# Two products change places in the order of a three-part matmul kernel, and three transposes move forward

## The chip, the cores and the metric

One core of one Trainium2 chip runs the whole program. The metric is the device time of one execution in microseconds (us); it is the median of several runs. Profiled executions are separate runs with the hardware profiler on, and every time inside the kernel is counted from the first instruction of such an execution.

## The reference

Three layers follow one another on 1536 tokens (2 batches of 768) with 512 features: a decayed linear attention, a mixture of 8 experts whose gate is normalised 8 times, and a dense layer with a leaky activation.

```python
state = gamma * state + einsum('bhd,bhe->bhde', k[:, :, t], v[:, :, t])   # attention, per token t
y[:, :, t] = scale * einsum('bhd,bhde->bhe', q[:, :, t], state)
...
for e in range(E):                                   # 8 experts, D 512, F 1024
    h = np.maximum(x @ w1[e], 0.0)
    out += P[:, e:e + 1] * (h @ w2[e])
...
h = x @ w_in                                         # dense layer, d_ff 2048
g = np.maximum(h, 0.0) + alpha * np.minimum(h, 0.0)
return g @ w_out
```

## The kernel before

After the attention the program is a list of 20 phases (`PHASES`). Phases 0 to 7 are the experts on the first batch. Phases 8 to 15 are the experts on the second batch, and 16 to 19 are the two halves of the dense layer on the first and on the second batch. Phases 8 to 19 are called fast in the code (`FAST`); below they are F1 to F12, so F1 to F8 are experts and F9 to F12 dense halves. The change touches fast phases alone. Each of them computes 1024 hidden units for 768 tokens and multiplies them with a second weight matrix.

The matrix products use a seven-product scheme (Strassen's, in Winograd's form): a 2x2 block product takes 7 products of half size. Each value is split in a high and a low part, so that every block multiplication is three matmuls, `L288`, `L289` and `L290` (`mm3`). A product of the first layer is `product(ph, j, p)`: block column `j` (0 to 3, 256 hidden units each) and product number `p` (1 to 7). It has two such triples, six matmuls of 128x384. The second layer is 28 units `u` (`fast2`), each also six matmuls.

The products of one column share four PSUM banks, A, B, D and E:

- 1 opens A. ScalarE (ACT) then copies A into B (`L934`), and product 6 adds onto that B.
- After 6, ACT copies B into a new bank E (`L934`), and then B into the SBUF block `b21` (`L934` too). Products 5 and, later, 3 add onto E.
- 7 opens D. ACT copies D into the SBUF block `b22` (`L934`), and product 4 later adds onto D.
- 2 adds onto A, and ACT turns A into `b11` (`L954`); 3 ends E, and ACT turns it into `b12` (`L954`). VectorE (DVE) adds E to `b22` after 5 and D to `b21` after 4 (`L949`). In the dense phases ACT writes `n` (`L905`) and DVE joins it (`L906`) in place of a ReLU.

DVE and ACT then make the operands of the second layer: `t1` to `t4` (`L1016`, `L1020`, `L1022`) combine blocks, `hhigh` (`L1042`, ACT) writes the high part of a tile `hs`, and `hlow` (`L1050` or `L1020`/`L1022`, DVE) its low part. There are 14 such `hs` tiles in a phase, and unit `u` reads number `u // 2`.

No scheduler reorders anything. A phase is a list of places (`sequence`): 26 from `fast_order`, then product 4 of column 3, unit 0, product 3 of column 3, and units 1 to 27. All other work is hung on places by number with `step(ph, place, ...)`, or on a product with `at(...)`, and follows that product's own work. So every engine has a fixed order, and each waits for the others by semaphores. All loads and stores are issued from one queue, SP's. The second layer's weights (`ws_load`, tile `ws`, 6 buffers) are loaded when the pair of units six tiles earlier has been issued.

In F1 alone, `turn` transposes the first batch's result (`total`) in eight pieces on TensorE (PE, 3 matmuls each, `L1161`), ACT copies each piece (`L1166`, tile `tt`) and SP stores it. `decode_at` turns weights that arrive as raw 64-bit words (`rd`, a load that SP issues) into floats on DVE (`L832` to `L837`, `L850`, `L853`).

Of the kernel before, what the change touches and what calls it, by code (L numbers as in the profile page):

```python
# [46 lines left out]
def tile_kernel(ctx, tc, lead, qkT, kv, ctab, w_gate, w1, w2, w_in, w_out, alpha, out):  # L47
# [69 lines left out]
    def w1_sum(n, q, eng):  # L117
        if n // NJ in AGAIN:
            return
        r = raw[0, n]  # L120
        s = r[:, 1024:1792].rearrange("p (a b) -> p a b", a=3)
        a11, a12, a22, a21 = (r[:, 256 * i:256 * i + 256] for i in range(4))
        out, in0, in1, op = (
            (s[:, 0], a21, a22, ALU.add),
            (s[:, 1], s[:, 0], a11, ALU.subtract),
            (s[:, 2], a21, a11, ALU.subtract),
            (a21, a12, s[:, 1], ALU.subtract),
        )[q]
        eng.tensor_tensor(out=out, in0=in0, in1=in1, op=op)  # L129

    def w1_adds(n, eng):
        if n < NJ * len(PHASES):
            for q in range(4):
                w1_sum(n, q, eng)

    def w1_high(n, part):
        kept = n // NJ in AGAIN
        if n >= NJ * len(PHASES) or kept and part == "c":
            return
        if part == "a":  # L140
            src, width, pieces = raw[0, n][:, 0:512], 512, (A11, A12)
        elif part == "b":
            width, pieces = (256, (A22,)) if kept else (512, (A22, W4))
            src = raw[0, n][:, 512:512 + width]
        else:
            src, width, pieces = raw[0, n][:, 1024:1792], 768, (W1, W2, W3)
        both = spot(n, part, 2 * width)
        hi, lo = both[:, 0:width], both[:, width:2 * width]
        nc.scalar.activation(out=hi, in_=src, func=AF.Copy)  # L149
        known = ws1.setdefault(n, {})  # L150
        known[part] = (lo, src, hi)
        for q, piece in enumerate(pieces):
            known[piece] = (hi[:, 256 * q:256 * q + 256], lo[:, 256 * q:256 * q + 256])

    def w1_low(n, part, eng):
        if n >= NJ * len(PHASES) or n // NJ in AGAIN and part == "c":
            return
        lo, src, hi = ws1[n].pop(part)
        eng.tensor_tensor(out=lo, in0=src, in1=hi.bitcast(F32), op=ALU.subtract)  # L159
        if part == "b" and n != 2 * NJ * E - 2:  # L160
            w_load(0, n + 2)
        if n < NJ * E and part != "a":
            unkept.append([2, n, part, hi, lo])
# [25 lines left out]
    def w2_high(n):  # L189
        hi, lo = (pools["wq"].tile([128, 1024], F32R, tag=f"v{n % NJ}{w}", name=f"v{n}{w}") for w in "hl")  # L190
        nc.scalar.activation(out=hi, in_=raw[1, n], func=AF.Copy)
        ws2[n] = (hi.rearrange("p (a b) -> p a b", a=2), lo.rearrange("p (a b) -> p a b", a=2))

    def w2_low(n, q, eng):
        hi, lo = (t[:, q, :] for t in ws2[n])
        eng.tensor_tensor(out=lo, in0=raw[1, n][:, 512 * q:512 * q + 512], in1=hi.bitcast(F32), op=ALU.subtract)
        if q == 1:
            w_load(1, n + 2)

    def w2_keep(n):  # L200
        e, j = divmod(n, NJ)
        for q in range(2):
            v = ws2[n][q].bitcast(F32).rearrange("p i (r c) -> p i r c", r=2)
            nc.sync.dma_start(out=c2[e][:, j, 0:2, q, :], in_=v[:, :, 0, :])
            nc.sync.dma_start(out=c2[e][:, j, 2, q, :], in_=v[:, 1, 1, :])
# [191 lines left out]
    with tc.manual_schedule():  # L397

        with ExitStack() as actx:
# [53 lines left out]
            pool, dve = nc.gpsimd, nc.vector  # L453
# [245 lines left out]
            for g in range(1, NST // 2):  # L699
                i = 2 * g  # L700
# [351 lines left out]
        def ws_load(ph, w):  # L1052
            if w >= 14:
                ph, w = ph + 1, w - 14
                if ph in XGROUP:
                    return
            if ph not in FAST:
                return
            x, jp = divmod(w, 2)
            t = wr[ph, w] = pools["fast"].tile([128, 2, 2, 256], F32R, tag="ws", bufs=6, name=f"ws{ph}_{w}")  # L1060
            nc.sync.dma_start(out=t.bitcast(F32), in_=c2[PHASES[ph][1]][:, 2 * jp:2 * jp + 2, PIECE2[ORDER2[x]]])
# [110 lines left out]
        def at(ph, key, *fns):  # L1172
            hooks.setdefault((ph, key), []).extend(fns)

        pool, dve = nc.gpsimd, nc.vector
# [3 lines left out]
        order += [(NJ - 1, 3), (NJ - 1, 4)]  # L1179
        slots = [f"t{t}{w}" for t in range(TT) for w in ("a", "")]  # L1180

        fast_order = [(0, 1), (0, 7), (0, 2), (0, 6), (0, 5)]
        for j in range(1, NJ):
            fast_order += [(j, 1), (j - 1, 4), (j, 2), (j, 6), (j - 1, 3), (j, 7), (j, 5)]

        def sequence(ph):
            if ph in FAST:
# [6 lines left out]
        def step(ph, pos, *fns):  # L1194
            if pos >= 60:
                ph, pos = ph + 1, pos - 60
            for fn in fns:
                at(ph, seq[ph][pos], fn)
# [20 lines left out]
        def w1_at(ph, m, add_eng, eng, adds, ah, al, ch, cl, bh, bl):  # L1219
            step(ph, adds, lambda: w1_adds(m, add_eng))  # L1220
            for part, hi, lo in (("a", ah, al), ("c", ch, cl), ("b", bh, bl)):
                step(ph, hi, lambda part=part: w1_high(m, part))
                step(ph, lo, lambda part=part: w1_low(m, part, eng))

        xk, x3 = [], []
        for ph in range(len(PHASES)):
            n = NJ * ph
# [25 lines left out]
                step(ph, 20, lambda m=n + 4: w1_kept(m))  # L1253
                step(ph, 26, lambda m=n + 5: w1_kept(m))
            if fast:
                w1_at(ph, n + 2, pool, dve, 0, 3, 4, 5, 7, 10, 11)
                w1_at(ph, n + 3, pool, dve, 5, 10, 12, 12, 14, 17, 18)
                w1_at(ph, n + 4, pool, dve, 28 if ph == 2 * E - 1 else 18, 36, 38, 39, 40, 42, 43)
                w1_at(ph, n + 5, pool, dve, 28, 44, 45, 48, 49, 50, 52)
            else:  # L1260
                if ph:
                    w1_at(ph, n + 2, pool, pool, 0, 3, 3, 6, 6, 9, 9)
                    w1_at(ph, n + 3, pool, pool, 5, 10, 10, 12, 12, 16, 16)
                else:
                    step(ph, 0, lambda: w1_adds(2, pool))
                    step(ph, 10, lambda: w1_adds(3, pool))
                    for m, part, hi, lo, eng in (
                        (2, "a", 5, 5, pool), (2, "c", 9, 9, pool), (2, "b", 11, 15, pool),
                        (3, "a", 13, 16, dve), (3, "c", 14, 14, pool), (3, "b", 17, 17, pool),
                        (4, "a", 25, 26, dve), (4, "c", 30, 31, dve), (4, "b", 37, 37, dve),  # L1270
                        (5, "a", 34, 34, dve), (5, "c", 34, 34, dve), (5, "b", 37, 37, dve),
                    ):
                        step(ph, hi, lambda m=m, part=part: w1_high(m, part))
                        step(ph, lo, lambda m=m, part=part, eng=eng: w1_low(m, part, eng))
                    for m, q, pos in ((4, 0, 22), (4, 1, 22), (4, 2, 24), (4, 3, 24), *((5, q, 31) for q in range(4))):
                        step(ph, pos, lambda m=m, q=q: w1_sum(m, q, dve))
                if ph > 0:
                    w1_at(ph, n + 4, dve, dve, 29, 29, 30, 31, 32, 31, 32)
                    w1_at(ph, n + 5, dve, dve, 33, 33, 34, 35, 36, 35, 36)
                early = ((4, 6, 7, dve), (9, 12, 13, dve), (15, 16, 20, dve), (22, 25, 26, dve))  # L1280
                first = ((6, 6, 7, dve), (12, 13, 14, dve), (20, 20, 20, pool), (24, 24, 24, pool))
                for j, (hi, l0, l1, eng) in enumerate(early if ph else first):
                    step(ph, hi, lambda m=n + j: w2_high(m))
                    step(ph, l0, lambda m=n + j, eng=eng: w2_low(m, 0, eng))
                    step(ph, l1, lambda m=n + j, eng=eng: w2_low(m, 1, eng))
                for j, pos in enumerate((19, 22, 29, 31)):
                    step(ph, pos, lambda m=n + j: w2_keep(m))
            if fast:
# [35 lines left out]
                if E < ph < 2 * E - 1:  # L1324
                    for keys in ((12, 17, 18, 27), (37, 39, 41, 45), (46, 48, 50, 55)):
                        i = unit[0] - NJ * E
# [21 lines left out]
        for w in range(6):  # L1348
            for ph in (E, 2 * E, 2 * E + 2):
                at(ph, ((0, 7), (1, 5), (1, 6), (1, 2), (2, 1), (2, 6))[w], lambda ph=ph, w=w: ws_load(ph, w))  # L1350
        for i, pos in enumerate((2, 4, 8, 11, 15, 18, 22, 25)):
            step(E, pos, lambda a=i % 4, h=i // 4: turn(2, a, h))
        def signs():
            dve.tensor_scalar(out=sg, in0=al, scalar1=1.0, scalar2=-2.0, op0=ALU.is_gt, op1=ALU.mult)
# [124 lines left out]
```

## Time and profile before

| | |
|---|---|
| median of 3 runs | 1285.64 us (1284.69 to 1285.79) |
| the profiled execution | 1288.47 us, of which the span from first to last instruction is 1286.7 us |
| PE busy in the span | 1261.4 us (98%) |
| DVE, ACT, POOL busy | 1011.5 us (79%), 659.6 us (51%), 459.5 us (36%) |
| fast phases | from 549.8 us to the end, about 60 to 65 us each |
| granted clock of PE | 0.998 of 2.4 GHz in the mean |

A row of the timeline gives the start of an instruction, its duration, engine, line, operation, output and inputs, and in square brackets the idle time of that engine before it and what ended it. Matmuls are pipelined: one is listed with some 0.33 us, but the next starts about 0.17 us after it. So idle time in brackets counts from the modelled end of the matmul before, and the pitch between starts says more.

### The profile page before, as it was taken

To read this page: it belongs to the slowest core of one execution; us is meant where nothing else is said; L and a number is where in the kernel's file an instruction comes from. 1 tells how busy PE (TensorE), PEld (TensorE's weight loads), DVE (VectorE), ACT (ScalarE), POOL (GpSimd) and SP (SyncE) were. 2 spreads that over 40 slices of the span, in tenths; PEclk is the share of its full clock that TensorE was granted. 3 is DMA by queue.
4 is the path that set the end of the run, shared out by engine and by line. 5 is a ranking of instruction groups with operands and counts; after the bars stand their busy time and mean duration, and the time that the engine had idled before them with its cause. 6 is when DMAs were issued, how large, how long until landed. Compare 5 with 4: busy or idle time off the path is not lost.

```text
span 1286.7 us, 20628 instructions
## 1 busy us (share of the span) xinstructions
PE 1261.4 (98%) x7358; PEld 1190.8 (93%) x7358; DVE 1011.5 (79%) x1546; ACT 659.6 (51%) x1217; POOL 459.5 (36%) x414
## 2 busy tenths in 40 slices
PE   9999999999999999999999999999999999999998
PEld 7889998989898989899999999999999989989998
DVE  6676888888898889758696777768685989797866
ACT  5634544444353535355545454646464556655573
POOL 5743252616170706001143413242322655543200
PEclk9999999999999999999999999999999999999999
DMA  9784999999999999899898989898988976596615
GB/s 359 242 287 134 330 333 343 337 339 337 332 341 343 337 346 334 289 334 350 299 357 277 346 280 342 291 351 280 348 280 293 352 237 207 188 350 221 218 46 180
DMA packets 231158, 379.21 MB, mean 295 GB/s; under 512 B 16992, under 2 KB 135824, under 8 KB 231056
## 3 DMA queue, kind: packets, MB, share of 16 engines
q1 hardware_dynamic: 231056, 377.90, 86.1%
q8 instruction: 58, 0.95, 0.3%
q14 instruction: 44, 0.36, 0.1%
HBM read 243.59 MB, written 132.67 MB: 292 GB/s over the span
## 4 chain that ended last, share of the span: by engine, by line
PE 84%; DVE 7%; DMA 3%; ACT 3%; issue 2%; SPq 0%; POOL 0%; DVEq 0%; ACTq 0%; POOLq 0%
PE B L289 7%; PE B L288 7%; PE o L288 7%; PE o L290 7%; PE B L290 7%; PE o L289 7%; PE A L288 6%; PE A L290 6%; PE A L289 6%; PE D L288 4%; PE D L290 4%; PE D L289 4%; PE E L288 4%; PE E L289 4%; PE E L290 4%
## 5 line engine op out<-in xcount | busy, mean ns | idle before, releaser
L129 POOL TENSOR_TENSOR raw<-raw 128x256 f32<-128x256 f32 x136 | 134.5, 1000 | 99.3 <-DMA raw<-in_w_dram 34.8
L1042 ACT ACTIVATE hs<-b 128x768 fp32r<-128x768 f32 x168 | 140.1, 842 | 58.0 <-DVE b L1020 14.9
L1050 DVE TENSOR_TENSOR hs<-b,hs 128x768 fp32r<-128x768 f32 x120 | 122.2, 1018 | 9.8 <-ACT hs L1042 9.5
L224 POOL TENSOR_TENSOR pr<-pr 128x256 f32<-128x256 f32 x52 | 51.2, 985 | 189.2 <-DMA pr<-in_w_dram 124.9
L149 ACT ACTIVATE W<-raw 128x512 fp32r<-128x512 f32 (+1 forms) x144 | 98.1, 695 | 19.8 <-DVE raw L129 19.3
L288 PE MATMUL A<-xh,W 128*128 128x384 f32 x320 | 108.0, 337 | 0.0
L290 PE MATMUL A<-xh,W 128*128 128x384 f32 x320 | 107.3, 335 | 0.0
L289 PE MATMUL A<-xl,W 128*128 128x384 f32 x320 | 107.1, 335 | 0.0
L357 POOL TENSOR_TENSOR xs<-b,xs 128x384 fp32r<-128x384 f32 x21 | 26.6, 1267 | 208.2 <-ACT xs L353 208.2
L289 PE MATMUL B<-hs,ws 128*128 128x384 f32 x288 | 97.0, 337 | 3.4 <-DVE hs L1050 3.3
L288 PE MATMUL B<-hs,ws 128*128 128x384 f32 x288 | 96.4, 335 | 0.2 <-ACT hs L1042 0.2
L290 PE MATMUL B<-hs,ws 128*128 128x384 f32 x288 | 96.3, 334 | 0.0
L1100 POOL TENSOR_TENSOR total<-total,t 128x384 f32<-128x384 f32 x54 | 69.6, 1318 | 64.6 <-DVE t L1080 61.5
L159 POOL TENSOR_TENSOR W<-raw,W 128x512 fp32r<-128x512 f32 (+1 forms) x49 | 76.3, 1572 | 41.7 <-PE B L290 20.7
L288 PE MATMUL B<-xh,W 128*128 128x384 f32 x268 | 90.8, 339 | 0.2 <-DVE D L972 0.2
L290 PE MATMUL B<-xh,W 128*128 128x384 f32 x268 | 89.7, 335 | 0.0
L289 PE MATMUL B<-xl,W 128*128 128x384 f32 x268 | 89.6, 334 | 0.0
L934 ACT ACTIVATE B<-A 128x384 f32<-128x384 f32 x48 | 22.8, 475 | 129.4 <-PE A L290 129.1
L267 POOL TENSOR_TENSOR dr<-dr 128x256 f32<-128x256 f32 x32 | 41.6, 1301 | 132.7 <-DMA xd<-tt 68.8
L288 PE MATMUL D<-xh,W 128*128 128x384 f32 x236 | 80.9, 343 | 7.7 <-ACT b L934 7.6
L159 DVE TENSOR_TENSOR W<-raw,W 128x512 fp32r<-128x512 f32 (+1 forms) x95 | 85.9, 920 | 2.3 <-ACT W L149 2.3
L949 DVE TENSOR_TENSOR b<-E,b 128x384 f32<-128x384 f32 x48 | 26.7, 556 | 72.4 <-PE E L290 67.5
(495 smaller groups left out, 3998.1 us busy)
## 6 DMA issues: line engine op xcount, KB each, us to landing
ws<-c SPq DMA_DIRECT2D x168, 512.0 KB, 5.9
raw<-in_w_dram SPq DMA_DIRECT2D x64, 512.0 KB, 5.6
c<-W SPq DMA_DIRECT2D x64, 384.0 KB, 6.6
W<-c SPq DMA_DIRECT2D x88, 256.0 KB, 6.0
pr<-in_w_dram SPq DMA_DIRECT2D x32, 512.0 KB, 5.7
c<-pw SPq DMA_DIRECT2D x32, 512.0 KB, 7.1
c<-pr SPq DMA_DIRECT2D x32, 512.0 KB, 7.7
raws<-in_w_dram SPq DMA_DIRECT2D x32, 384.0 KB, 4.8
```

The lines of the kernel that those rows point to most:

```text
L129: eng.tensor_tensor(out=out, in0=in0, in1=in1, op=op)
L149: nc.scalar.activation(out=hi, in_=src, func=AF.Copy)
L159: eng.tensor_tensor(out=lo, in0=src, in1=hi.bitcast(F32), op=ALU.subtract)
L224: eng.tensor_tensor(out=out, in0=in0, in1=in1, op=op)
L267: nc.gpsimd.tensor_tensor(out=out, in0=in0, in1=in1, op=op)
L288: nc.tensor.matmul(ps, ah, bh, start=first, stop=False, skip_group_check=True)
L289: nc.tensor.matmul(ps, ah, bl, start=False, stop=False, skip_group_check=True)
L290: nc.tensor.matmul(ps, alo, bh, start=False, stop=last, skip_group_check=True)
L949: nc.vector.tensor_tensor(out=dst, in0=src, in1=dst, op=ALU.add)
L1042: nc.scalar.activation(out=t[:, 0, :], in_=hsource(ph, k), func=func)
L1050: nc.vector.tensor_tensor(out=lo, in0=src, in1=hi.bitcast(F32), op=ALU.subtract)
L1100: eng.tensor_tensor(out=dst, in0=dst, in1=tt[m, h], op=ALU.add)
```

## The change

In column 0 the products come as 1 7 6 2 5 in place of 1 7 2 6 5. In column 3, product 7 comes ahead of product 3 of column 2, which now stands directly ahead of product 5. (The general line is changed and columns 1 and 2 are put back as they were by the two swaps.) The split of column 2's first weight pieces (those of products 1 and 2) into high and low part moves one place later, from places 3 and 4 to 4 and 5; the place that it writes to is read by column 0's product 2, which now stands at place 3. Places count from 0. In F1, the last three of the eight transposes move from places 18, 22 and 25 to 17, 20 and 22.

```diff
-        fast_order = [(0, 1), (0, 7), (0, 2), (0, 6), (0, 5)]
+        fast_order = [(0, 1), (0, 7), (0, 6), (0, 2), (0, 5)]
         for j in range(1, NJ):
-            fast_order += [(j, 1), (j - 1, 4), (j, 2), (j, 6), (j - 1, 3), (j, 7), (j, 5)]
+            fast_order += [(j, 1), (j - 1, 4), (j, 2), (j, 6), (j, 7), (j - 1, 3), (j, 5)]
+        fast_order[9], fast_order[10] = fast_order[10], fast_order[9]
+        fast_order[16], fast_order[17] = fast_order[17], fast_order[16]
...
-                w1_at(ph, n + 2, pool, dve, 0, 3, 4, 5, 7, 10, 11)
+                w1_at(ph, n + 2, pool, dve, 0, 4, 5, 5, 7, 10, 11)
...
-        for i, pos in enumerate((2, 4, 8, 11, 15, 18, 22, 25)):
+        for i, pos in enumerate((2, 4, 8, 11, 15, 17, 20, 22)):
```

On ACT, at the start of F2 (phase 9 in the names; A, B, D, E are banks, `b_9` the SBUF blocks), the order changes like this:

```order
 L934 ACTIVATE B_6655<-A_6648 128x384
 L934 ACTIVATE b_9_6674<-D_6667 128x384
-L954 ACTIVATE b_9_6682<-A_6648 128x384
-L934 ACTIVATE E_6691<-B_6655 128x384
-L934 ACTIVATE b_9_6693<-B_6655 128x384
-L149 ACTIVATE W<-raws 128x512
...
+L934 ACTIVATE E_6682<-B_6655 128x384
+L934 ACTIVATE b_9_6684<-B_6655 128x384
+L954 ACTIVATE b_9_6693<-A_6648 128x384
+L149 ACTIVATE W<-raws 128x512
```

The two copies out of B after product 6, into E and into `b21`, now come ahead of the ReLU of product 2.

On ACT, at the end of F2's first layer (`hs_1` and `hs_4` are high parts for the second layer, the row with D is the copy into `b22` after product 7, the rows with E are ReLUs after product 3):

```order
 L934 ACTIVATE E_6900<-B_6864 128x384
 L934 ACTIVATE b_9_6819<-B_6864 128x384
-L1042 ACTIVATE hs_4_6903<-b_9_6682 128x768
-L954 ACTIVATE b_9_6911<-E_6817 128x384
+L1042 ACTIVATE hs_4_6903<-b_9_6693 128x768
+L934 ACTIVATE b_9_6835<-D_6905 128x384
 L1042 ACTIVATE hs_1_6913<-b_9_6809 128x768
-L934 ACTIVATE b_9_6835<-D_6915 128x384
-L954 ACTIVATE b_9_6911<-E_6900 128x384
+L954 ACTIVATE b_9_6921<-E_6817 128x384
+L954 ACTIVATE b_9_6921<-E_6900 128x384
```

The copy of D moves ahead of one high part, and the ReLU of column 2's product 3 goes behind it.

On DVE, at the end of F9's first layer (phase 16, a dense one; `n_01` is what ACT writes for product 3, `b_16_11101` is `b22`):

```order
 L906 SCALAR_TENSOR_TENSOR b_16_11079<-b_16_11079,sg,n_10_11141 128x384
-L906 SCALAR_TENSOR_TENSOR b_16_11175<-E_11077,sg,n_01_11176 128x384
-L1050 TENSOR_TENSOR hs_4_11165<-b_16_10914,hs_4_11165 128x768
+L1050 TENSOR_TENSOR hs_4_11165<-b_16_10924,hs_4_11165 128x768
 L949 TENSOR_TENSOR b_16_11101<-E_11160,b_16_11101 128x384
+L906 SCALAR_TENSOR_TENSOR b_16_11186<-E_11077,sg,n_01_11187 128x384
 L1022 TENSOR_TENSOR b_16_11001<-b_16_10904,b_16_11001 128x768
```

The join for column 2's product 3 moves from ahead of the low part of `hs_4` to behind the sum of `b22`.

## Rows read from the trace of the kernel before

**Rows 1.** Windows of F1, F2, F8, F10: length, busy of PE, PEld, DVE, ACT, POOL, clock, DMA share.
```profile
549.80:613.40 63.60, 61.55 (x362) 60.64 (x361) 45.36 (x69) 33.91 (x63) 4.71 (x4) 1.00 1.00 353
613.40:673.30 59.90, 58.95 (x338) 58.30 (x337) 47.64 (x67) 31.80 (x58) 14.96 (x12) 1.00 0.93 327
...
973.00:1036.00 63.00, 59.90 (x339) 58.30 (x338) 49.21 (x64) 31.88 (x56) 28.57 (x23) 1.00 0.84 294
...
1098.00:1163.00 65.00, 61.35 (x337) 59.40 (x336) 55.29 (x69) 38.26 (x69) 29.95 (x28) 0.97 0.76 274
```

**Rows 2.** Waits of PE: who waited for whom, us in total, times, longest.
```profile
PE D L288 <- ACT b L934: 7.6, 11, 1.8
PE E L288 <- ACT E L934: 6.9, 12, 0.6
PE B L289 <- DVE hs L1050: 3.3, 3, 1.7
```

**Rows 3.** Timeline of F2's first products on PE and ACT.
```profile
617.40 0.34 PE L290 MATMUL B<-xh,W 128*128 128x384 f32 x1
...
617.77 0.47 ACT L934 ACTIVATE E<-B 128x384 f32<-128x384 f32 x1 [0.55 <-PE B L290]
...
618.30 0.44 PE L288 MATMUL E<-xh,W 128*128 128x384 f32 x1 [0.56 <-ACT E L934]
...
619.46 0.34 PE L288 MATMUL A<-xh,W 128*128 128x384 f32 x1
...
620.51 0.33 PE L288 MATMUL D<-xh,W 128*128 128x384 f32 x1
```

**Rows 4.** Timeline of F2's last column: ACT, then the matmul that waits.
```profile
639.51 0.85 ACT L1042 ACTIVATE hs<-b 128x768 fp32r<-128x768 f32 x1 [0.21 <-DVE b L1020]
640.27 0.47 ACT L954 ACTIVATE b<-E 128x384 f32<-128x384 f32 x1
640.64 0.84 ACT L1042 ACTIVATE hs<-b 128x768 fp32r<-128x768 f32 x1
641.38 0.48 ACT L934 ACTIVATE b<-D 128x384 f32<-128x384 f32 x1
...
641.91 0.44 PE L288 MATMUL D<-xh,W 128*128 128x384 f32 x1 [0.39 <-ACT b L934]
```

**Rows 5.** Timeline of F1: DVE behind a load, ACT behind DVE, PE.
```profile
572.35 0.43 DVE L832 TENSOR_SCALAR ex<-rd 128x512 uint32<-128x512 uint32 x1 [4.30 <-DMA rd<-in_w_out_dram]
...
579.26 0.85 ACT L1042 ACTIVATE hs<-b 128x768 fp32r<-128x768 f32 x1 [1.56 <-DVE b L1020]
...
582.03 0.44 PE L288 MATMUL D<-xh,W 128*128 128x384 f32 x1 [1.48 <-ACT b L934]
```

**Rows 6.** Timeline of F8 on PE: column 3's product 4, a later unit.
```profile
1000.84 0.34 PE L290 MATMUL E<-xh,W 128*128 128x384 f32 x1
1001.25 0.45 PE L288 MATMUL D<-xh,W 128*128 128x384 f32 x1
...
1030.89 0.45 PE L289 MATMUL B<-hs,ws 128*128 128x384 f32 x1 [1.68 <-DVE hs L1050]
```

**Rows 7.** Timeline of F9: DVE joins product 3, PE starts product 4.
```profile
1064.34 0.62 DVE L906 SCALAR_TENSOR_TENSOR b<-E,sg,n 128x384 f32<-128x384 f32 x1 [0.74 <-ACT n L905]
...
1065.47 0.45 PE L288 MATMUL D<-xh,W 128*128 128x384 f32 x1 [1.12 <-ACT b L934]
```

**Rows 8.** Timeline of F10: PE, DVE, and PE at a late unit.
```profile
1128.19 0.45 PE L288 MATMUL D<-xh,W 128*128 128x384 f32 x1 [1.81 <-ACT b L934]
...
1136.55 0.96 DVE L1050 TENSOR_TENSOR hs<-b,hs 128x768 fp32r<-128x768 f32 x1 [1.08 <-ACT hs L1042]
...
1159.08 0.45 PE L289 MATMUL B<-hs,ws 128*128 128x384 f32 x1 [0.95 <-DVE hs L1050]
```

**Rows 9.** Window of F10, columns as in Rows 1.
```profile
1129.00:1132.00 3.00, 3.00 (x11) 3.00 (x11) 3.00 (x5) 1.23 (x2) 2.92 (x3) 0.50 1.03 410
```

**Rows 10.** Loads of the second layer's weights, all phases: issue to landing.
```profile
DMA to landing us min/median/max: 3.3/5.9/8.8
```

## Prediction

> **What bounds the kernel now.** I read the page first, then a table of windows, one for each fast phase, then the waits of PE, and last the timeline around each wait. In F2's 59.9 us PE is busy 58.95 and DVE 47.64, and the page has PE at 98% with no other engine above 79%; so time can be won only where PE stands still, or runs slowly as in F10, with a mean clock of 0.97 [rows 1]. The waits of PE say where it stands: in two places of nearly every fast phase [rows 2]. The one is a first matmul onto E that waits for ACT's copy into E, 12 times, 6.9 us in all. The other is a matmul onto D that waits for ACT's copy out of D, 11 times, 7.6 us. A third kind, units of the second layer behind DVE, comes 3 times.
>
> The timeline gives the true price of such a wait. In F2 the last matmul of product 6 starts at 617.40 and product 5 starts at 618.30 [rows 3]. Six matmuls take 1.05 (619.46 to 620.51), so the pitch is 0.175, and 0.90 minus 0.175 is 0.73 lost. Product 5 itself then takes 1.16 (618.30 to 619.46) where a product takes 1.05, which is 0.11 more. One wait costs 0.84: the 0.56 of idle in brackets and 0.28 that the bracket does not count. I add 0.27 to every bracket; the 0.39 ahead of F2's product 4 [rows 4] is 0.66.
>
> **The change part by part.**
>
> *Column 0: product 6 ahead of product 2.* Product 5 needs the copy into E. ACT starts it 0.2 after PE is done with product 6, and PE goes on 0.73 after that point [rows 3]. Now product 2 stands between and covers 1.05, so the wait goes and 0.3 is left over. The ReLU of product 2 goes behind the copy on ACT, so nothing new lies ahead of it. The price is on product 6: it adds onto B, ACT's copy of A after product 1. That copy had two products as cover (7 and 2) and now has one, 7. By the timing of the copy into E, 0.73 against 1.05, one is enough. I cost it at nothing; if that cover fell short by the whole, it would be 0.84 again. Gain: 6.9 + 12 x 0.27 = 10.1 us.
>
> *Column 3: product 7 ahead of product 3.* Product 4 waits for the copy of D into `b22`. In F2 that copy is the last of four on ACT: a high part at 639.51 that waited for DVE, the ReLU at 640.27, a second high part at 640.64, the copy at 641.38 [rows 4]. In the new order the copy stands behind the first high part, at about 640.3, and frees D at about 640.8. Without its wait PE would be there at 641.91 - 0.55, about 641.35. So the wait goes, with 0.5 to spare. The second high part stays within 0.1 of its time, and the ReLU that goes behind it is not needed before the next product 3. F2 to F7, F11 and F12 have the same order and no other wait. Their brackets are the 7.6 less the three long ones, 1.48, 1.12 and 1.81 [rows 5, 7, 8], which leaves 3.2 for eight; with 8 x 0.27 that is a gain of 5.35 us.
>
> The other four phases are bound differently at this place.
>
> - F1: DVE stood 4.30 behind a load that landed at 572.35, and ACT's first high part waited for DVE until 579.26 [rows 5]. The window's DMA share is 1.00 [rows 1], so I expect the load at nearly the same time though PE comes 0.84 earlier. Then ACT does the high part (0.75), one transposed piece (0.4) and the copy of D (0.5), by [rows 4] and taking the piece like the ReLU. So product 4 starts at about 580.9, not 582.03: 1.1 for both waits of F1, and up to 1.95 if the load moves with PE. I take 1.5: 0.84, counted above, and 0.67 here. The three transposes are the same work in other places. One piece lies ahead of the copy now as before, so I cost them at nothing; if it fell badly it would cost its own 0.4.
> - F8: PE goes from 1000.84 to 1001.25, 0.41 for 0.175, and loses the 0.11 behind it: 0.34 [rows 6]. DVE's work for the later units hangs on product 3, so it moves with PE. Gain 0.34. The wait of 1.68 at 1030.89 stays, since DVE has the same work in a row ahead of it.
> - F9: the wait is 1.12 + 0.27 = 1.39 [rows 7]. But DVE is the next bound. It stood 0.74 at 1064.34 for ACT's `n` of product 3. In the new order ACT has a split, the copy, a high part and `n` to do first, about 2.05 (0.4, 0.4, 0.75, 0.5 by the ACT rows), and DVE meanwhile a low part and a sum, about 1.5. So DVE stands about 0.5 there, and all that follows on it is only 0.2 earlier. Gain 0.2, with bounds 0 and 1.39.
> - F10: the wait is 1.81 + 0.27 [rows 8]. Behind it the granted clock is 0.50, 1.2 GHz and not 2.4 [rows 9]. At half the clock 12 matmuls at twice the pitch lose up to 2.1; I count 1.8. In the new order the copy comes about 1.1 earlier (0.75 and 0.4 as above), so 0.7 of the bracket remains, and the clock should hold. Most of this is not won: at 1159.08 PE still waits for DVE [rows 8], which is busy 55.3 of F10's 65.0 us [rows 1]. DVE's one long stop, 1.08 at 1136.55, is for ACT, which waited for PE's slow stretch; it shrinks by some tenths. Gain 0.5, with bounds 0 and 3.9.
>
> *The sum.* 10.1 + 5.35 + 0.67 + 0.34 + 0.2 + 0.5 = 17.2 us. The profiled execution took 1288.47, 1.8 more than its span and 2.8 more than the median. It becomes 1271.3, and the median 1285.64 - 17.2 = 1268.4 us.
>
> Two things move beside it and cost nothing. The split of column 2's first weights is one place later on ACT and DVE, at places 4 and 5, and is first read at place 12; without these 7 us of room it would be ACT's and DVE's half microsecond each. On SP's queue three stores of transposed pieces in F1 go ahead of a raw load, of a store with a load, and of two stores. PE waits for none of these now [rows 2]; if the load behind one held DVE as the one at 572.35 does, it would be some 0.4 us, once.
>
> **The rivals.**
>
> *All is won.* If F1's load moves with PE, and DVE follows in F9 and F10, then 1.08, 1.19, 1.58 and the clock's 1.8 are added: 22.9 gained, 1262.8 us. Against it speaks that DVE's work in F9 and F10 has few gaps to give.
>
> *The change does not do what it says.* The wait for E only turns into one of product 6 for B, at the same 0.84. Then the first 10.1 is lost: 1278.5 us. For it speaks that the cover halves; against it that a copy takes 0.73 of 1.05. Its mirror, the copy of D still late, loses the other 7.1: 1275.5 us.
>
> *New idle time drops the clock.* In F9 and F10 PE runs ahead and then waits for DVE in several units, about 1 us each. If one of these ends like the 1.81, it costs up to 1.8, in one or two phases: 1270 to 1272 us. Against it: F8's wait of 1.68 [rows 6] left its clock at 1.00 [rows 1].
> The Trainium skill has such a rule ("TensorE: Matmul & The Clock Gate", A second HAM failure mode: psum-queue depth-cycling): frequent small idles of PE between groups of matmuls make the clock swing between its levels. By that rule this rival would be the likely one; in the trace, F1 and F2, with two waits each, show no swing.
>
> *DMA becomes the bound, and the kernel is slower.* F1 has a DMA share of 1.00 and F2 0.93 [rows 1]. With shorter phases the loads of the second layer's weights could land later. They have six buffers for tiles of two units, so a load is issued ten units ahead, 10.5 us; the longest landing was 8.8, the median 5.9 [rows 10]. If landing rose to 12 us, six tiles would take 14.1 in place of 12.6, and a phase's 14 tiles would lose 3.5; over F1 to F7 that is 24.5 us against 17.2 gained, 1293 us. It decides from a landing of 11.55 us on. Against it: F2's DMA work is 0.93 x 59.9 = 55.7 us, and the phase becomes 58.4.
>
> **How the numbers follow.** Forecast: 0.73. All won: 0.09. One of the two halves fails: 0.07. Clock: 0.06. DMA: 0.03. No change for a reason that I don't see: 0.02. A measurement of this kernel tells about 0.2%, 2.6 us, from no change. The first four cases are faster by more, so faster 0.95, same 0.02, slower 0.03. The forecast's own bounds are F1 (0.4 either way), F8 to F10 (1 less, 2 more) and some tenths in each of the plain phases (2 less): 1266 to 1272. The range of 8 in 10 takes in the clock's case with some room above it, and the near part of "all won": 1264.5 to 1273.5. It leaves out the failed half, DMA, no change and the far end of "all won".
>
> **What would show it.** In the waits of PE the row of E behind ACT should be gone, and that of D shrink from 7.6 to about 2, all in F1 and F10. F2 to F7 should be 58.4 us long, not 59.9. F10 should show no clock of 0.50, and PE's waits for DVE should grow from 3.3 to 5 or more. I am wrong if product 6 waits for ACT, if F2 to F7 stay above 59, or if F9 and F10 shorten by the whole of their waits.

## Result and profile after

The changed kernel takes 1271.53 us (1271.01 to 1273.27), the kernel before in the same session 1285.66 us. The medians differ by 14.1 us; the ratio of the runs is 0.9894 (0.9877 to 0.9911), which is 11.4 to 15.8 us. Forecast were 17.2 us and 1268.4, with a range of 1264.5 to 1273.5: the time lies in the range, and the gain is 3 us short of the sum, by more than the noise.

| | before | after |
|---|---|---|
| profiled execution / its span | 1288.47 / 1286.7 us | 1271.30 / 1269.6 us |
| PE busy | 1261.4 us (98%) | 1256.4 us (99%) |
| DVE, ACT, POOL busy | 1011.5, 659.6, 459.5 us | 1010.1, 656.3, 460.8 us |

The windows of F1, F2, F3, F8, F9 and F10 after, with the columns of [rows 1]:

```profile
548.40:609.80 61.40, 61.38 (x362) 60.78 (x361) 44.67 (x67) 33.93 (x63) 4.75 (x4) 1.00 1.01 359
609.80:668.40 58.60, 58.60 (x338) 58.30 (x337) 47.04 (x66) 31.48 (x58) 16.28 (x12) 1.00 0.95 336
668.40:727.80 59.40, 59.01 (x338) 58.23 (x337) 46.15 (x64) 30.77 (x57) 22.76 (x18) 1.00 0.93 318
961.90:1023.90 62.00, 59.25 (x338) 58.29 (x337) 49.39 (x64) 31.65 (x56) 28.43 (x23) 1.00 0.84 300
1023.90:1085.00 61.10, 60.45 (x339) 58.18 (x338) 55.20 (x67) 40.57 (x75) 35.74 (x31) 1.00 0.78 252
1085.00:1148.90 63.90, 60.34 (x337) 57.99 (x336) 55.64 (x69) 38.20 (x69) 30.34 (x28) 1.00 0.77 279
```

F2 went from 59.90 to 58.60 with PE busy all the time; F3 got stuck at 59.40, and F8 to F10 stay 2.5 to 5.3 us above F2. The clock is 1.00 in each. The waits of PE after, against [rows 2]:

```profile
PE B L289 <- DVE hs L1050: 4.0, 4, 1.6
PE D L289 <- DVE hs L1050: 1.1, 2, 0.6
PE D L288 <- ACT b L934: 0.7, 1, 0.7
PE E L289 <- DVE hs L1020: 0.5, 1, 0.5
PE E L288 <- ACT E L934: 0.3, 1, 0.3
PE A L289 <- DVE hs L1050: 0.3, 1, 0.3
```

The 12 waits for E, all in column 0, are gone; the one listed is new, in column 2 of F3. Of the 11 for D one is left, and no product 6 waits for B. Waits for DVE grew from 3.3 to 5.9. In new executions of the same two kernels (experiments 1 and 9) they grew from 4.3 to 6.1, and a second wait for D was left, 1.02 in F1.

F2's first products on PE and ACT, against [rows 3]: the last matmul of product 6, product 2, ACT's copy into E, and products 5 and the next column's 1.

```profile
612.74 0.33 PE L290 MATMUL B<-xh,W 128*128 128x384 f32 x1
612.91 0.33 PE L288 MATMUL A<-xh,W 128*128 128x384 f32 x1
...
613.11 0.47 ACT L934 ACTIVATE E<-B 128x384 f32<-128x384 f32 x1 [0.55 <-PE B L290]
...
613.95 0.33 PE L288 MATMUL E<-xh,W 128*128 128x384 f32 x1
...
614.99 0.33 PE L288 MATMUL A<-xh,W 128*128 128x384 f32 x1
```

The copy ends at 613.58, 0.37 ahead of product 5 (0.3 forecast), and product 5 takes 1.04, without the slow start. F2's last column, against [rows 4]:

```profile
635.58 0.85 ACT L1042 ACTIVATE hs<-b 128x768 fp32r<-128x768 f32 x1 [0.75 <-DVE b L1020]
...
636.33 0.47 ACT L934 ACTIVATE b<-D 128x384 f32<-128x384 f32 x1
...
636.70 0.34 PE L290 MATMUL E<-xh,W 128*128 128x384 f32 x1
...
636.87 0.42 PE L288 MATMUL D<-xh,W 128*128 128x384 f32 x1
```

The copy of D follows the first high part and ends at 636.80. Product 4 starts at 636.87, at the normal pitch, and only its second matmul is 0.09 late. But 0.07 is to spare and not 0.5: the high part, which waits for DVE, came 1.29 ahead of product 4 in place of 2.40, so DVE is less early than PE. The reason is a raw load in F2, behind which DVE stands; the row before and the row after:

```profile
631.79 0.43 DVE L832 TENSOR_SCALAR ex<-rd 128x512 uint32<-128x512 uint32 x1 [1.33 <-DMA rd<-in_w_in_dram]
```

```profile
628.37 0.43 DVE L832 TENSOR_SCALAR ex<-rd 128x512 uint32<-128x512 uint32 x1 [2.39 <-DMA rd<-in_w_in_dram]
```

Counted from F2's start, DVE goes on at 18.40 before and at 18.60 after, and works from there without a stop until the high part can start, while PE is 0.84 earlier from product 5 on. In F4 to F7, F11 and F12 of the same profile the copy of D ends 0.40 to 0.80 ahead of product 4, as forecast.

F1, against [rows 5]: DVE behind the load, ACT's high part, the copy of D, product 4.

```profile
569.81 0.43 DVE L832 TENSOR_SCALAR ex<-rd 128x512 uint32<-128x512 uint32 x1 [3.89 <-DMA rd<-in_w_out_dram]
...
576.72 0.85 ACT L1042 ACTIVATE hs<-b 128x768 fp32r<-128x768 f32 x1 [0.88 <-DVE b L1020]
577.47 0.47 ACT L1166 ACTIVATE tt<-tr 128x384 f32<-128x384 f32 x1
577.84 0.48 ACT L934 ACTIVATE b<-D 128x384 f32<-128x384 f32 x1
...
578.38 0.45 PE L288 MATMUL D<-xh,W 128*128 128x384 f32 x1
```

From DVE's start behind the load to product 4 it is 8.57 us, where it was 582.03 - 572.35 = 9.68. The 1.11 between them is the forecast's 1.1.

Phases F1 to F12, from PE's first matmul of one to that of the next (of F12, to the start of its last matmul). The second pair are experiments 1 and 9:

| | forecast gain | before, after | gain | second executions | gain |
|---|---|---|---|---|---|
| F1 | 1.51 | 63.74, 61.41 | 2.33 | 63.56, 62.37 | 1.19 |
| F2 | 1.51 | 59.90, 58.62 | 1.28 | 59.88, 58.74 | 1.14 |
| F3 | 1.51 | 59.94, 59.38 | 0.56 | 59.95, 58.88 | 1.07 |
| F4 | 1.51 | 59.95, 58.56 | 1.39 | 59.92, 58.46 | 1.46 |
| F5 | 1.51 | 59.97, 58.50 | 1.47 | 59.97, 58.93 | 1.04 |
| F6 | 1.51 | 59.94, 58.50 | 1.44 | 59.94, 58.77 | 1.17 |
| F7 | 1.51 | 59.96, 58.64 | 1.32 | 59.92, 58.46 | 1.46 |
| F8 | 1.18 | 62.88, 61.98 | 0.90 | 62.90, 62.00 | 0.90 |
| F9 | 1.04 | 62.17, 61.00 | 1.17 | 62.19, 60.99 | 1.20 |
| F10 | 1.34 | 65.22, 63.96 | 1.26 | 64.87, 64.39 | 0.48 |
| F11, F12 | 3.02 | 119.41, 116.65 | 2.76 | 119.44, 116.54 | 2.90 |
| sum | 17.15 | 733.08, 717.20 | 15.88 | 732.54, 718.53 | 14.01 |

The profiled spans differ by 17.1, but 1.3 of that lies ahead of the first phase, which the change does not touch, and some 0.35 more is the clock of F10 in that one execution (65.22 with its fall, 64.87 without). The second pair agrees with the medians.

### The profile page after: what moved, and what is told of

The parts are those of the page before. It is cut to its first block, busy times and chain, and to the rows that moved or that the text cites. A ratio compares the mean times of both kernels' runs of the same rounds, so it can differ in the third digit from the quotient of the medians.

```text
span 1269.6 us, 20641 instructions
## 1 busy us (share of the span) xinstructions
PE 1256.4 (99%) x7358; PEld 1189.3 (94%) x7358; DVE 1010.1 (80%) x1546; ACT 656.3 (52%) x1217; POOL 460.8 (36%) x414
## 4 chain that ended last, share of the span: by engine, by line
PE 85%; DVE 8%; DMA 4%; issue 1%; ACT 1%; SPq 1%; POOL 0%; DVEq 0%; POOLq 0%; ACTq 0%
PE B L289 7%; PE B L288 7%; PE B L290 7%; PE o L288 6%; PE o L290 6%; PE o L289 6%; PE A L289 6%; PE A L288 6%; PE A L290 6%; PE D L290 4%; PE D L289 4%; PE D L288 4%; PE E L288 4%; PE E L289 4%; PE E L290 4%; DVE hs L1050 1%
## 5 line engine op out<-in xcount | busy, mean ns | idle before, releaser
L357 POOL TENSOR_TENSOR xs<-b,xs 128x384 fp32r<-128x384 f32 x21 | 29.1, 1384 | 196.5 <-ACT xs L353 196.5
```

The lines of the kernel that those rows point to most:

```text
L357: eng.tensor_tensor(out=t[:, 1], in0=src[q], in1=t[:, 0].bitcast(F32), op=ALU.subtract)
```

## Experiments

**1 to 4: the parts.** Experiment 1 is the kernel before once more. The others are the kernel before with one part each: column 0 alone (with the weight split's places), the last column alone, the transposes alone.

```diff
 # experiment 2
-        fast_order = [(0, 1), (0, 7), (0, 2), (0, 6), (0, 5)]
+        fast_order = [(0, 1), (0, 7), (0, 6), (0, 2), (0, 5)]
-                w1_at(ph, n + 2, pool, dve, 0, 3, 4, 5, 7, 10, 11)
+                w1_at(ph, n + 2, pool, dve, 0, 4, 5, 5, 7, 10, 11)
 # experiment 3: product 7 of column 3 ahead of product 3 of column 2
 # experiment 4
-        for i, pos in enumerate((2, 4, 8, 11, 15, 18, 22, 25)):
+        for i, pos in enumerate((2, 4, 8, 11, 15, 17, 20, 22)):
```

> The kernel before, unchanged, profiled a second time. Open: the trace became 17.1 us shorter (span 1286.7 to 1269.6), the median 14.1 us. Theory: the profiled execution of before was a long one, because of the fall of the clock in F10 and a later start of the fast phases (549.65 against 548.36); a second trace of the same kernel then has a span of about 1284 us, F10 near 63.5 us without a clock of 0.50, and the fast phases starting near 548.4. Rival: the trace was typical and the 3 us are lost or won outside of it; then the span is again about 1286.7 with the clock fall in F10. Time against before: the same, within 0.1%.

> Only column 0 in the order 1 7 6 2 5 (with the split of column 2's first weights one place later). Theory: the wait for the copy into E goes in all 12 phases at 0.84 each, 10.1 us, less what F1, F9 and F10 give back because their next bound is a load or DVE: 8 to 10 us faster (ratio 0.992 to 0.994). PE's wait for E behind ACT is gone, that for D behind ACT stays at about 6 to 8 us. Rival: the two waits hang on each other, and the wait for D grows by what the wait for E shrinks; then the gain is under 3 us.

> Only product 7 ahead of product 3 in the last column. Theory: the wait for the copy of D goes in the eight plain phases and F8 (5.7 us) and partly in F1, F9 and F10 (about 1.4 us): 6 to 7.5 us faster (ratio 0.994 to 0.9955). PE's wait for E behind ACT stays at 6.9 us. Rival: the copy is late because of DVE, which the order does not change; then PE's wait for D stays above 5 us and the gain is under 2 us.

> Only the last three transposes of F1 moved forward. Theory: the same work in other places, with one piece ahead of the copy of D as before: within 0.3 us of before, F1's wait for D stays between 1.2 and 1.7 us. Rival: the pieces hold up ACT's row of copies in F1, and F1's larger gain (2.33 us where 1.5 was forecast) comes from them; then F1 alone is 0.5 to 1 us shorter here.

| | median, us | ratio to before |
|---|---|---|
| 1 before again | 1286.15 | 1.0001 (0.9992 to 1.0010) |
| 2 column 0 alone | 1279.00 | 0.9935 (0.9923 to 0.9946) |
| 3 last column alone | 1279.64 | 0.9945 (0.9934 to 0.9957) |
| 4 transposes alone | 1286.09 | 0.9998 (0.9990 to 1.0007) |

The kernel before had a median of 1286.23 in the same session. The two orders give 7.2 and 6.6 by the medians, in sum 13.8 where the whole gives 14.1; by the ratios it is 8.4 and 7.1, 15.4 where the whole gives 13.6. Within the noise of 1 to 2 us the parts add up. The waits of PE in experiment 1, and then in experiment 2:

```profile
PE D L288 <- ACT b L934: 7.4, 11, 1.8
PE E L288 <- ACT E L934: 6.9, 12, 0.6
```

```profile
PE D L288 <- ACT b L934: 9.3, 11, 1.9
```

All of E's 6.9 is gone, but the wait for D grew by 1.9, most of it in F2 to F7: there PE arrives earlier where ACT is not as much earlier. So in these phases a part of column 0's gain is handed on, unless the last column goes with it. What each part alone takes off the phases of experiment 1:

| | F1 | F2 to F7, each | F8 | F9 | F10 | F11, F12 |
|---|---|---|---|---|---|---|
| 2 column 0 alone | 0.26 | 0.32 to 0.88 | 0.90 | 0.86 | 1.07 | 1.83 |
| 3 last column alone | 1.63 | 0.57 to 0.61 | 0.04 | 0.33 | 0.00 | 0.96 |

In F8, F9, F11 and F12 column 0 gives its 0.84 or a little more by itself. The last column gives next to nothing in F8 and F10. There the wait for D shrinks and comes back as waits for DVE. In F10 of experiment 3, the wait that shrank and one that grew:

```profile
1118.74 0.44 PE L288 MATMUL D<-xh,W 128*128 128x384 f32 x1 [0.58 <-ACT b L934]
...
1129.10 0.44 PE L289 MATMUL D<-hs,ws 128*128 128x384 f32 x1 [0.55 <-DVE hs L1050]
```

In experiment 1 the first was 1.79 and the second 0.34. (Of the 1.63 in F1, about 1.0 is an earlier load, as experiment 12 will show.)

In experiment 1 the span was 1284.1 and the clock did not fall in F10, as I had said, but F10 took 64.87 and not 63.5. In experiment 4 F1's wait for D was 0.23 and not the 1.2 to 1.7 that I had said, and F1 was 1.1 to 1.3 shorter; experiment 12 returns to that.

**5: how much cover a copy needs.** In column 0 product 6 directly behind product 1.

```diff
-        fast_order = [(0, 1), (0, 7), (0, 6), (0, 2), (0, 5)]
+        fast_order = [(0, 1), (0, 6), (0, 7), (0, 2), (0, 5)]
```

> The changed kernel with column 0 in the order 1 6 7 2 5, so that product 6 follows product 1 at once and has no product as cover for ACT's copy of A into B. My theory: the copy takes 0.73 us of PE's time from the end of the product that it copies, and one product (1.05) covers it wholly. Then here a row of PE for B behind ACT appears, 12 times at about 0.56 (6.7 in all), the price is 0.84 each, 10 us in the 12 phases, and the time goes to about 1281. The rival, that the order among ACT's instructions and not the cover decides (ACT does the copy while PE's queue still runs): no such row and a time within 2 of the changed kernel's 1271.5.

1280.01 us, 0.9950 (0.9936 to 0.9963): 7.9 above the changed kernel's order in the same session (experiment 6, 1272.07), where I had said 10. One row of the waits of PE, and from the timeline of F2 the end of product 1, ACT's copy of A into B, and product 6:

```profile
PE B L288 <- ACT B L934: 6.8, 12, 0.6
```

```profile
610.66 0.34 PE L290 MATMUL A<-xh,W 128*128 128x384 f32 x1
611.04 0.47 ACT L934 ACTIVATE B<-A 128x384 f32<-128x384 f32 x1 [10.31 <-PE A L290]
611.57 0.44 PE L288 MATMUL B<-xh,W 128*128 128x384 f32 x1 [0.56 <-ACT B L934]
```

Without cover the copy costs the same 0.56 in brackets in all 12 phases, here 0.91 from matmul to matmul; with one product as cover nothing (in F2 after, the copy ends at 611.50 and product 6 starts at 611.87). That settles the rival on product 6: it is a true price, and the order 1 7 6 avoids it.

**6 and 9: is F3's 59.4 in the order?** In F3 after, ACT stood 3.13 for a load ahead of a split, and PE got its E late:

```profile
685.77 1.06 ACT L253 ACTIVATE dw<-dr 128x1024 fp32r<-128x1024 f32 x1 [3.13 <-DMA dr<-wd]
...
687.11 0.48 ACT L934 ACTIVATE E<-B 128x384 f32<-128x384 f32 x1
```

Experiment 6 moves that split in F1 to F7; experiment 9 is the changed kernel once more.

```diff
-                    for pos, fn in zip((6, 12, 24, 27, 40, 52), dense_prep(ph - E)):
+                    for pos, fn in zip((6, 17, 24, 27, 40, 52), dense_prep(ph - E)):
```

> The changed kernel with one piece of other work moved: the split of the dense layer's prepared weights, which waits for its load on ACT (3.13 us in F3 of the changed kernel), stands at place 17 in place of 12. My theory: this wait alone keeps F3 at 59.4 us where its neighbours take 58.5, because ACT's copy of B into E comes late in column 2; so F3 falls to 58.6, the wait for E at 687.6 goes, F1, F2 and F4 stay as they are, and the time falls by 0.8, less than is told apart by the medians. The rival, that F3 is long by DVE's work or by transfers: F3 stays at 59.3 or more.

> The changed kernel once more, unchanged, for another profiled execution. My theory by now: F1, F2 and F3 differ from one execution to the next by up to 1 us each, with the time at which a load lands behind which DVE or ACT stands (in F1 the raw weights rd, in F2 and F3 dr), so that the 61.4, 58.6 and 59.4 of the first profile are one draw. Then at least one of the three differs here by 0.4 or more, with the landing, while F4 to F7, F11 and F12 repeat within 0.1 (58.5, 58.5, 58.5, 58.6, 58.5, 58.2). The rival, that F3's 59.4 is a property of the order (the split at place 12): F3 is 59.3 to 59.5 again. Time 1271.5.

Experiment 6: 1272.07 us, the same. F3 fell to 58.62 as I had said, but F1 took 62.42 and F2 59.50, so the sum of the three rose by 1.1. In F2, DVE stood behind the raw load again, longer than in the first profile:

```profile
629.39 0.43 DVE L832 TENSOR_SCALAR ex<-rd 128x512 uint32<-128x512 uint32 x1 [3.29 <-DMA rd<-in_w_in_dram]
```

The wait for D then came back in F2 with 0.30; in experiment 8, where DVE stood 2.92, with 0.82 (F2 59.63). Experiment 9: 1272.41 us, and without any edit F1 took 62.37, F2 58.74 and F3 58.88. So 59.4 was mostly one draw of when loads land, and experiment 6 alone would have misled me. My statement that F4 to F7 repeat within 0.1 fell too: F5 and F6 came out at 58.93 and 58.77. In F5 DVE and then PE of experiment 9, at product 3 of column 3:

```profile
815.72 0.55 DVE L949 TENSOR_TENSOR b<-E,b 128x384 f32<-128x384 f32 x1
```

```profile
815.88 0.34 PE L290 MATMUL A<-hs,ws 128*128 128x384 f32 x1
816.32 0.45 PE L288 MATMUL E<-xh,W 128*128 128x384 f32 x1
```

Product 3 adds onto E, which DVE's sum still reads until 816.27. In the first profile this sum came 0.45 earlier in the phase, and only 0.07 was lost there. By as much, ACT stood longer for the load `dr` in F5: 2.72 here, 2.27 there. The forecast had no such wait.

**12: F1 and the transposes.** The changed kernel with the transposes where they were before.

```diff
-        for i, pos in enumerate((2, 4, 8, 11, 15, 17, 20, 22)):
+        for i, pos in enumerate((2, 4, 8, 11, 15, 18, 22, 25)):
```

> The changed kernel with the last three transposes of F1 put back to places 18, 22 and 25. My theory: F1's length is set by the landing of the raw weights rd and not by the transposes; so F1 is as long as its landing says (the landing counted from F1's start, plus 40.0 us, give or take 0.2: 61.4 for 21.4, 62.4 for 22.4), and the time is within 1 of the changed kernel's 1271.5. The rival, that the moved transposes are what brought F1 from the 62.2 that I forecast to 61.4 (alone they gave 1.1 to 1.3 in the trace): the landing is the same and F1 is at least 0.5 longer than the landing says, and the time is 0.8 to 1.3 higher.

1271.78 us, 0.9884 (0.9869 to 0.9899), the same as the changed kernel. F1 took 62.30 with the load 22.35 behind F1's start. Set side by side, DVE's start behind this load (the L832 row, counted from F1's start) and F1's length:

| old last column | landing, F1 | new last column | landing, F1 |
|---|---|---|---|
| before | 22.70, 63.74 | after | 21.45, 61.41 |
| experiment 1 | 22.48, 63.56 | experiment 9 | 22.45, 62.37 |
| 2, column 0 | 22.26, 63.29 | 12, old transposes | 22.35, 62.30 |
| 4, transposes | 21.40, 62.47 | 6, split | 22.48, 62.42 |
| 7 | 23.34, 64.39 | 8 | 22.19, 62.13 |
| 10 | 23.24, 64.32 | 11 | 22.88, 62.80 |

On the left F1 is the landing plus 41.03 to 41.08 in all six, on the right plus 39.92 to 39.96. The transposes and column 0 change nothing in it; the last column gives 1.1. Experiment 5, the new last column with 22.92 and 62.86, fits the right side too. (Experiment 3, 21.48 and 61.93, lies 0.5 above it: it still has E's wait, and PE came 0.59 later than the copy of D.) The 1.1 to 1.3 us that experiment 4 seemed to win in F1 were its landing at 21.40. Why the load lands between 21.4 and 23.3 was not tried.

**7, 8, 10, 11: what keeps the gain in F9 and F10.** The forecast put it on DVE. Experiments 7 and 8 take work from DVE all over these two phases (it makes only 32 columns of the low parts of the first layer's weights), 10 and 11 at one place (two joins write 32 columns), each in the kernel before and in the changed one. The other columns are left unwritten.

```diff
 # 7 (before), 8 (after)
-        eng.tensor_tensor(out=lo, in0=src, in1=hi.bitcast(F32), op=ALU.subtract)
+        w = 32 if 16 * NJ + 2 <= n < 18 * NJ + 2 else lo.shape[1]
+        eng.tensor_tensor(out=lo[:, 0:w], in0=src[:, 0:w], in1=hi[:, 0:w].bitcast(F32), op=ALU.subtract)
 # 10 (before), 11 (after), in leaky
+            w = 32 if i and j == 3 and n // NJ in (2 * E, 2 * E + 1) else HT
-                    out=dst, in0=src, scalar=sg[:, f:f + 1], in1=t, op0=ALU.mult, op1=ALU.max
+                    out=dst[:, 0:w], in0=src[:, 0:w], scalar=sg[:, f:f + 1], in1=t[:, 0:w], op0=ALU.mult, op1=ALU.max
```

> The kernel before with less work for DVE in F9 and F10: of the low parts of the first layer's weights that are prepared for these two phases, DVE makes only the first 32 of 512 columns, the others stay unwritten (PE multiplies all the same). It is the partner of the next run, and shows what F9 and F10 take in the old order when DVE is not the bound. My theory: the waits of PE for ACT in column 3 (1.12 and 1.81) stay about as they are, since they hang on ACT's order, the waits for DVE in the later units go, F9 is about 61.5 and F10 about 62 to 63; time about 1282. The rival, that those waits hang on DVE too: they shrink to 0.4, and F9 and F10 take 60.0 like the plain phases; 1279.

> The changed kernel with the same relief for DVE in F9 and F10. My theory of the prediction was that DVE keeps most of the gain of these two phases. With DVE light, the change should give there what was withheld: F9 58.6 to 59.5 and F10 59 to 60.5, against 61.0 and 63.9 in the changed kernel with all of DVE's work, and the time about 5 us below it, 1266 to 1267. The rival, that these phases are long by something else (ACT's work, PE's six more matmuls, transfers): F9 and F10 stay above 60.5 and 63, and the time is within 1.5 of 1271.5.

> The kernel before with DVE's chain at the end of the first layer shortened in F9 and F10: the two joins for column 3's products 5 and 4 write 32 of 384 columns, the others stay without the leaky activation; about 1.8 us less for DVE in each phase, at that place alone. Partner of the next run. My theory: in the old order PE stands for ACT's copy of D ahead of these joins and not for DVE behind them, so F9 stays at 62.0 to 62.2 and F10 loses at most some tenths from 64.9; time 1285 to 1286. The rival, that any DVE work taken away in F9 or F10 shortens them in either order: F9 61.2 or less.

> The changed kernel with the same two joins shortened in F9 and F10. My theory: what DVE keeps of the change's gain there is kept by this chain (sum, low part, two joins, join, t1, then ACT's high part and DVE's low part, for which PE waits 0.55 at the third pair of units), not by DVE's load in the phase as a whole. With the joins short that wait goes: F9 falls by 0.9 to 60.1, and F10, where two waits of 0.55 and 0.73 hang on it, by 1.2 to 2 to 62 to 62.8; against the kernel before with the same joins the change then gives 2 in F9 and 2 to 3 in F10, where it gave 1.2 and 0.9 to 1.3. The rival, that the load as a whole is what counts: F9 and F10 fall by as much as in the kernel before with short joins, and the change's gain there stays near 1.2.

| | median, us | ratio to before | F9, F10 | gain there |
|---|---|---|---|---|
| before, after (second executions) | | | 62.19, 64.87; 60.99, 64.39 | 1.20, 0.48 |
| 7, 8: light | 1283.33, 1269.25 | 0.9977 (0.9968 to 0.9986), 0.9866 (0.9848 to 0.9883) | 61.06, 63.01; 59.90, 61.88 | 1.16, 1.13 |
| 10, 11: joins short | 1285.77, 1271.77 | 0.9990 (0.9979 to 1.0001), 0.9886 (0.9872 to 0.9901) | 61.68, 65.23; 60.49, 63.34 | 1.19, 1.89 |

Both theories fell. With DVE light F9's gain stayed at 1.16, and F9 took 59.90, between the two cases that I had named; with the joins short F9's gain was 1.19 and not 2. In the old order the waits and F9 did not stay as I had said either. The window of F9 in experiment 8:

```profile
1023.70:1083.60 59.90, 59.32 (x338) 58.24 (x337) 45.95 (x67) 40.77 (x75) 33.90 (x32) 1.00 0.82 272
```

With 9 us less for DVE in F9 (45.95 for 55.20) the phase is 1.1 shorter, but in the old order as well, and the change's gain in F9 stays at 1.2. So DVE's load in the phase is not what holds the change's gain back; in experiment 7 it made the waits for the copy of D shorter too (0.71 and 1.31, where they were 1.12 and 1.79 in experiment 1). Shorter joins cut F9 by 0.5 in either order. Only F10's gain rose, and 0.4 of that or so is the clock, which fell in experiment 10's F10 and not in 11's.

What holds back can be read behind the column. F9 after, on PE (product 4, then a unit of the third pair) and on DVE, against [rows 7]:

```profile
1051.43 0.45 PE L288 MATMUL D<-xh,W 128*128 128x384 f32 x1
...
1061.16 0.45 PE L289 MATMUL D<-hs,ws 128*128 128x384 f32 x1 [0.55 <-DVE hs L1050]
```

```profile
1052.61 0.62 DVE L906 SCALAR_TENSOR_TENSOR b<-E,sg,n 128x384 f32<-128x384 f32 x1 [0.43 <-ACT n L905]
...
1055.43 2.11 DVE L906 SCALAR_TENSOR_TENSOR b<-b,sg,n 128x384 f32<-128x384 f32 x2
...
1058.10 1.14 DVE L1016 TENSOR_TENSOR b<-b,b 128x768 f32<-128x768 f32 x1
1060.15 0.96 DVE L1050 TENSOR_TENSOR hs<-b,hs 128x768 fp32r<-128x768 f32 x1 [0.91 <-ACT hs L1042]
```

Product 4 hardly waits any more: of the 1.40 that PE lost there, counted as all time over the pitch, 0.20 is left. DVE then works from 1052.61 to t1's end without a stop, and PE stands for it at the third pair of units, where it now loses 1.16 with the slow starts and lost 0.26 before. So 0.85 + 1.40 - 0.20 - 0.90 = 1.15, the measured 1.17. Experiment 3 shows the last column's share by itself: DVE's stop at the join is 0.43 there too, 0.31 less than before, and F9 is 0.33 shorter. In experiment 11 the same t1 (L1017 there), on DVE and then POOL's work at that time:

```profile
1057.23 1.84 DVE L1017 TENSOR_TENSOR b<-b,b 128x768 f32<-128x768 f32 x1
```

```profile
1057.24 1.02 POOL L357 TENSOR_TENSOR xs<-bb,xs 128x384 fp32r<-128x384 f32 x1
```

The short joins saved 1.23 on DVE, but t1, which started with POOL's L357, took 1.84, and PE's wait only fell from 0.55 to 0.38. That this collision is what kept the rest is read from the trace; a version with POOL's instruction elsewhere was not run.

## Why the prediction was right, and where it was off

- **Column 0.** As forecast: E's waits went in all 12 phases, 0.37 to spare against 0.3, product 6 pays nothing. The price of 0.84 for a bare copy holds (experiment 5).
- **The plain eight.** Forecast 12.1 us, won 10.2 in either pair. F4, F7 and F12 come to within 0.2 of their 1.51 in both; F2, F3, F5 and F6 lose up to 0.95 of it in one execution or another. The term was mis-sized. That "the wait goes, with 0.5 to spare" was worked out on F2's rows. It held in F4 to F7, F11 and F12 of the first profile, but not in F2, where 0.07 was left: it takes ACT's first high part and PE as they stood, though column 0 brings PE 0.84 earlier. That is right where the high part comes earlier too, and in F2 it hangs on DVE, which stands for a raw load. That these phases "have the same order and no other wait" left out two more, product 3 for E behind DVE's sum, and ACT behind a late load.
- **F1.** The bound of 1.1 was right, and the choice of 1.5 a little high. The load does not follow PE; it lands at its own time, which differs by 1.9 us between executions. The 2.33 of the first pair was 1.1 of order and 1.25 of landing.
- **F8.** Its column gave the 0.34, but at a later unit the wait for DVE grew from 0.14 to 0.47, so 0.90 was won in place of 1.18. With the last column alone (experiment 3) it is the same: 0.46 there, and 0.04 won. "DVE's work for the later units moves with PE" failed for that one unit.
- **F9.** 1.17 and 1.20 against 1.04: DVE's stop at the join shrank from 0.74 to 0.43 (0.5 forecast), and the rest came back as a wait at a unit, as the step said. Its reason, that DVE's chain behind the join comes only a little earlier, holds (experiment 3); DVE's share of the phase is no reason (experiment 8). That a shorter chain would let more through is not shown: experiment 11 cut the chain and the gain stayed.
- **F10.** 0.5 to 1.3 against 1.34. Of the wait 0.73 remained, as forecast (0.7), and the clock holds. But the term of 0.5 was not there: the last column alone won 0.00 (experiment 3 against 1, neither with a fall of the clock); that the first pair's 1.26 lies near 1.34 is luck. A new wait of 0.29 for DVE appeared, and one grew from 0.34 (experiment 1) to 0.55. The clock's loss that I took from [rows 9] is not there in every execution, and where it is, F10 is only 0.35 longer (65.22 against 64.87), not 1.8: the waits of 0.34 and 0.74 for DVE, which follow in experiment 1, are not there behind the slow stretch. The rows of PE after, against [rows 8]:

```profile
1112.91 0.44 PE L288 MATMUL D<-xh,W 128*128 128x384 f32 x1 [0.73 <-ACT b L934]
...
1117.88 0.44 PE L289 MATMUL A<-hs,ws 128*128 128x384 f32 x1 [0.29 <-DVE hs L1050]
...
1123.29 0.44 PE L289 MATMUL D<-hs,ws 128*128 128x384 f32 x1 [0.55 <-DVE hs L1050]
1128.45 0.45 PE L289 MATMUL B<-hs,ws 128*128 128x384 f32 x1 [0.73 <-DVE hs L1050]
...
1144.67 0.44 PE L289 MATMUL B<-hs,ws 128*128 128x384 f32 x1 [0.97 <-DVE hs L1050]
```

- **The sum.** 17.2 against 14.1 (14.0 in the second executions): about 1.8 of the 3.1 in the plain eight, 0.9 in F10, 0.3 each in F1 and F8, and F9 0.2 the other way.
- **The rivals.** Product 6 does not wait. "All is won" failed in F1, F9 and F10; its sum was also too high, as it gives F1 2.59 where the bound set ahead of it was 1.95. No new idle time dropped the clock: the waits of 0.97 and, in F8, 1.65 left it at 1.00. The swing that the Trainium skill reports for frequent small idles of PE ("TensorE: Matmul & The Clock Gate", A second HAM failure mode: psum-queue depth-cycling) was not seen in the changed kernel. DMA's share rose to 1.01 in F1, and loads did cost tenths in F2, F3 and F5. The second layer's weights landed as before (longest 8.5 us, it was 8.8; median 6.1, it was 5.9), far from the 11.55 that the DMA rival needs.

## What to carry to other kernels

Price a wait from start to start of the matmuls, and then ask who is next: a removed wait is worth its whole price only where the engine behind it also comes earlier, and it is partly handed on where that engine hangs on a load or on a full chain of its own. Where a phase stands behind a load, as F1 does here, its length is the landing plus a constant; only the constant belongs to the change. Slack that was worked out on the rows of one phase is to be looked up in the others too, and an engine that stands for a load does not come earlier with the rest. Two profiles of the same kernel, phase by phase, show which differences are the order and which are one execution.

## What the runs showed of the hardware that was not expected

- **The clock after the same wait.** In the old last column PE stands about 1.8 us in F10. Behind it the granted clock fell to 0.50 in the profile of before (1.81), in experiment 2 (1.93) and in experiment 10 (1.79), and did not in experiments 1 and 4 (1.79 each). The windows of 3 us from product 4 on, in experiment 10 and then in experiment 1:

```profile
1126.40:1129.40 3.00, 3.00 (x11) 3.00 (x12) 3.00 (x5) 1.14 (x3) 2.48 (x3) 0.63 1.04 417
```

```profile
1125.90:1128.90 3.00, 3.00 (x17) 3.00 (x18) 3.00 (x5) 1.14 (x3) 2.48 (x3) 1.00 1.03 415
```

The other engines do the same in both; 11 matmul records against 17. What decides it is open.

- **DVE behind POOL.** t1 on 768 columns takes 0.96 alone (F10 after, at 1120.40). In F9 it took 1.14 in the changed kernel, 1.84 in experiment 11 and 1.59 in experiment 10, and each time it ended 0.81 or 0.82 after the end of POOL's L357 (1058.42, 1058.26, 1069.75), whenever it had begun. The 1.14 was there before the change as well (at 1071.24), so the change did not bring this collision. The Trainium skill ("SBUF — State Buffer", SBUF: two separate sides) says that DVE with two SBUF inputs and a GpSimd instruction that reads SBUF exclude each other for a whole instruction; these three rows agree. In experiment 11 DVE is listed 0.01 ahead of POOL and still ends behind it, so the rows do not tell who goes first.
